# An attention and expert kernel whose 1,080 steps are issued in another written-down order

## The chip, the cores and the metric

The kernel runs on one core of one Trainium2 chip. The metric is device time in microseconds (us), the median of three runs.

## What is computed

Eight batches; in each, eight heads of 576 tokens with 64 channels go through two attentions, whose results are added, and the sum goes through a layer in which 128 chosen tokens pass an expert.

```python
def _attn_ref(q, k, v):
    # q_d, k_d, v_d: means over groups of 4 tokens (144 left)
    out_up = np.repeat(softmax(scale * q_d @ k_d.T) @ v_d, 4, axis=2)
    # every token attends to the tokens less than 4 places away
    scores = np.where(abs(pos[:, None] - pos[None, :]) < 4, scale * q @ k.T, -1e9)
    return out_up + softmax(scores) @ v

def _moe_ref(x, w_gate, w1, w2, capacity):     # x: 8 x 576 x 512
    scores = x @ w_gate
    for b in range(8):
        top = the 128 tokens of b with the highest scores
        out[b, top] = x[b, top] + sigmoid(scores[b, top]) * (relu(x[b, top] @ w1) @ w2)
```

## The kernel before

The work is cut into 1,080 steps. A step belongs to one engine (PE, DVE, ACT, POOL, or SP for loads and stores) and emits a few instructions. `Plan.add` collects them batch by batch, `Plan.given` (L216) reads the table `ORDER` (L40), and `Plan.emit` emits the steps in that order. Every engine takes its instructions strictly in the order in which they were emitted, and so does each queue of transfers. So the table decides, engine by engine, what stands behind what. The entry `54+4` is step 54 with four idle matmuls ahead of it (`idle`, L269): products of an identity matrix into the step's own bank, which no result uses. Since the table is there, the planner in `Plan.order` does not run, and the numbers that the steps carry (times in ns, `key`, `size`) have no effect.

One batch b goes through these parts:

- **Loads.** `load_qk` loads q and k (`T`, two transfers of 1152 KB, two buffers in turn) and DVE sums groups of four (`dT`). `load_vw` loads the windows of v (`vw`), `pool_v` loads v once more (`vraw`) and POOL sums it.
- **Coarse attention** (`coarse`, L513). PE makes scores (`sd`), ACT the exponentials (`ed`, `er`), PE turns them (`pspd`, `pspr`) and multiplies (`od`, step `products`), DVE scales (`ods`), SP writes that to memory (`up_d`) and reads it back spread fourfold into `up`, one transfer step for each of five tiles j.
- **Local attention** (`local`, L676), in three pieces k of two, two and one tiles. PE makes scores (`sl`), DVE the maxima (`mx`, `mb`), PE subtracts them (`sl` out of `minus`), ACT the exponentials (`ex`), PE turns them (`pspl`), ACT copies (`pt`), PE multiplies (`ol`), DVE divides (`t`), POOL adds `up` (`t` out of `t,up`), DVE takes the gate's sum (`jk`), SP stores the tokens (`out_dram` out of `t`).
- **Route** (`route`, L859). With all five sums there (`scp`), PE spreads them (`sb`), DVE compares (`beat`) and PE counts (`cb`), DVE writes the choice (`oh`), PE picks the indices (`pi`), DVE makes them whole numbers (`idx`). Then POOL issues a gather of the 128 chosen rows from memory (`xe` out of `out_dram,idx`, L933); it needs `idx` and the landed stores of that batch. PE turns the rows (`px`), ACT and DVE split them into two halves (`xeh`, `xel`).
- **Experts** (`experts`, L965). PE multiplies by w1 (`ph`, 96 matmuls in eight steps), ACT and DVE cut and split (`hh`, `hl`), PE multiplies by w2 (`py`, 24 matmuls in eight steps), DVE adds (`xe` out of `py`), POOL scatters the rows back.

The weights come once: eight loads into `stg` (two buffers in turn, shared with `w_gate`), each split by ACT (`w1h`, `w2h`) and DVE (`w1l`, `w2l`); a load waits until DVE has done with the buffer's load before. All instructions of steps stand under line L89, since the wrapper there records them; so they are told apart by their tiles.

```python
for st in self.given() if ORDER else self.order():
    for b in st.makes:
        b.tile = b.make()
    for _ in range(st.fills):
        self.idle(st.fill)
    st.emit()
```

Of the kernel before, what the change touches and what calls it, by code (L numbers as in the profile page):

```python
# [21 lines left out]
P = 128  # L22
# [15 lines left out]
ACCUM, OT = True, False  # L38
BIASED = (2,)
ORDER = """  # L40
# [38 lines left out]
"""  # L79


# [41 lines left out]
class Plan:  # L123
# [11 lines left out]
    def add(self, engine, ns, key, emit, r=(), w=(), uses=(), claims=(), after=(), size=0, lock=False, fill=None, soft=()):  # L135
        step = Step(engine, ns, key, emit, r, w, uses, claims, after, size, lock, fill, soft)
        self.steps.append(step)
        return step
# [94 lines left out]
def tile_multires_attention_moe(ctx: ExitStack, tc: tile.TileContext, qk, vw, vp, cs, w_gate, w1, w2, outs):  # L233
# [8 lines left out]
    DM = H * D  # L242
# [34 lines left out]
    add = plan.add  # L277
# [4 lines left out]
    def small(tag, shape, dtype=F32):  # L282
        return Buf(tag, 3, lambda: sm.tile(list(shape), dtype, tag=tag, name=tag))

    def two_banks(name):
        return Buf("psA", 2, lambda: psA.tile([P, 2, 512], F32, tag="A", name=name))
# [5 lines left out]
    def fixed(t):  # L292
        b = Buf(None, 1, None)
        b.tile = t
        return b
# [33 lines left out]
    out_d = [fixed(None) for b in range(B)]  # L329
# [346 lines left out]
    def local(b, k, key):  # L676
        tiles = TU[k]
        T, vl, sc = Ts[b], vws[b][k], scs[b]
        ns = len(tiles)
        ng = ns * HP  # L680
        s = two_banks("sl")
# [43 lines left out]
        mx = small("mx", [P, 2, UL * HP])  # L725
        mb = None if biased else small("mb", [P, 2, UL * HP], BF16)
        given = biased and ACCUM
        dn = small("dn", [P, 2, UL * HP]) if given else None
        ex = sbuf("ex", [P, UL * HP, 2 * KW], 2)
# [31 lines left out]
        def row_exps(i):  # L761
            for g in range(HP * i, HP * (i + 1)):
                for a in range(2):
                    act.activation(
                        ex[:, g, KW * a : KW * (a + 1)], s[:, a, KW * g : KW * (g + 1)], AF.Exp,
                        bias=mx[:, a, g : g + 1], scale=scale, **({"accum_out": dn[:, a, g : g + 1]} if given else {}),
                    )
            if given and i == ns - 1:
                act.activation(dn[:, :, :ng], dn[:, :, :ng], AF.Copy, bias=EPS)
# [5 lines left out]
        if biased:  # L775
            add("ACT", 200, key, negative, r=[mx], w=[mx])
            for i in range(ns):
                add("ACT", (2325 + 190 * (i == ns - 1)) if given else 1592, key + 0.004 * i, lambda i=i: row_exps(i), r=[s, mx], w=[ex, dn] if given else [ex])
            row = ex.writers[:]
            if given:  # L780
                add("DVE", 165, key + 0.01, inverse, r=[dn], w=[dn])
        else:
            add("DVE", 95, key, low, r=[mx], w=[mb], lock=True)
            add("PE", 20 + 425 * ns, key, shift, r=[mx, mb, minus], w=[s])
            add("ACT", 60 + 440 * ns, key, exps, r=[s], w=[ex])
            row = ex.writers * ns
# [72 lines left out]
    def route(b, key):  # L859
# [59 lines left out]
        pi = bank("T" if b == B - 1 else "F", "pi")  # L919

        def pick():
            for j in range(NT):
# [7 lines left out]
        idx, gs = small("idx", [P, 1], I32), small("gs", [P, 1])  # L930
        add("DVE", 70, key + 0.02, lambda: vec.tensor_copy(idx.tile, pi[:, 0:1]), r=[pi], w=[idx])
        xe = sbuf("xe", [P, DM], 3)
# [1 line left out]
            "POOL", 1050, key + 0.02,  # L934
            lambda: pool.indirect_dma_start(
                out=xe.tile, out_offset=None, in_=x_d[b], in_offset=bass.IndirectOffsetOnAxis(ap=idx.tile, axis=0),
            ), r=[idx, out_d[b]], w=[xe], size=P * DM * 4,
        )
        def gates():
            act.activation(gs.tile, pi[:, 1:2], AF.Exp, scale=-1.0)  # L940
            act.activation(gs.tile, gs.tile, AF.Copy, bias=XS * WS * WS, scale=XS * WS * WS)

        add("ACT", 240, key + 0.03, gates, r=[pi], w=[gs])
        add("DVE", 165, key + 0.04, lambda: vec.reciprocal(gs.tile, gs.tile), r=[gs], w=[gs])
        px = bank("T", "px")

# [157 lines left out]
```

## Time and profile before

| | |
|---|---|
| median of three runs | 295.74 us (294.67 to 295.88) |
| the profiled execution | 297.18 us |
| its span, first to last instruction | 295.40 us |
| PE busy | 252.6 us, 86% |
| DVE busy | 218.1 us, 74% |
| ACT, POOL busy | 134.8 us, 126.7 us |
| moved by DMA | 70.4 MB, 238 GB/s over the span |
| mean granted TensorE clock | 0.975 |

The profile shows one execution, instruction by instruction. The windows view gives each engine's busy time in a stretch, the granted TensorE clock (1.00 is 2.4 GHz, 0.50 is 1.2 GHz) and the busy share of the 16 DMA engines. A timeline gives one engine's instructions with the idle time ahead of them and what ended it. The chain of waits is the work that ended last, followed back from the end. The profiled execution is 1.44 us above the median, 0.5%.

### The profile page before, as it was taken

The numbers are of one execution on the slowest core, as the hardware profiler recorded it, in microseconds if no ns is written. First come the engines' busy times: TensorE is split into PE (matmuls) and PEld (weight loads), VectorE is DVE, ScalarE is ACT, GpSimd is POOL, SyncE is SP. The second block draws the span as 40 slices with busy tenths as digits, with TensorE's granted clock in tenths as the row PEclk, the third lists the DMA queues.
The fourth block names the chain that finished last, engine by engine and source line by source line (L and its number), as shares of the span: only waits on it lengthen the run. The fifth ranks groups of instructions, "written<-read, shape, count | busy, mean of one in ns | idle before, by whom it ended". The sixth has DMA issues, their size and how long they took to land.

```text
span 295.4 us, 11752 instructions
## 1 busy us (share of the span) xinstructions
PE 252.6 (86%) x5000; PEld 184.0 (62%) x5000; DVE 218.1 (74%) x466; ACT 134.8 (46%) x474; POOL 126.7 (43%) x160
## 2 busy tenths in 40 slices
PE   3887896686499797999989759999999999997892
PEld 0654564464287467867775548867865787693571
DVE  2888798778489888988888888689895885387211
ACT  0388665364355544286415633645347453620110
POOL 6055838474212668255572731157414521082201
PEclk9999999759889999999999999999999999999999
DMA  7999986787959989987984897857837462645200
GB/s 229 387 416 359 350 307 194 251 285 243 345 185 314 273 305 358 306 311 224 329 291 157 249 366 246 299 167 187 285 121 224 136 170 73 198 117 165 71 2 36
DMA packets 27195, 70.40 MB, mean 238 GB/s; under 512 B 5864, under 2 KB 8040, under 8 KB 24328
## 3 DMA queue, kind: packets, MB, share of 16 engines
q1 hardware_dynamic: 25864, 65.47, 66.3%
q0 software_dynamic: 1280, 4.20, 4.1%
q8 instruction: 39, 0.64, 0.9%
q14 instruction: 12, 0.10, 0.1%
HBM read 55.76 MB, written 13.89 MB: 236 GB/s over the span
## 4 chain that ended last, share of the span: by engine, by line
PE 39%; DMA 16%; issue 8%; DVE 6%; SPq 4%; ACT 3%; POOL 2%; POOLq 0%; DVEq 0%; ACTq 0%
PE ph L89 8%; PE py L89 7%; DMA up<-up_d 7%; PE sl L89 6%; DMA xe<-out_dram,idx 5%; SPq L89 4%; PE ol L89 4%; PE od L89 4%; PE pspl L89 3%; POOL t L89 2%; ACT ex L89 2%; PE sd L89 2%; PE pspd L89 2%; DMA vw<-in_vw_dram 2%; PE sb L89 2%
## 5 line engine op out<-in xcount | busy, mean ns | idle before, releaser
L89 POOL TENSOR_TENSOR t<-t,up 128x512 f32<-128x512 f32 x40 | 50.2, 1272 | 56.6 <-DMA up<-up_d 35.9
L89 PE MATMUL ph<-xel,w1h 128*128 128x128 f16 x256 | 44.2, 219 | 0.5 <-DVE xel L89 0.5
L89 PE MATMUL ph<-xeh,w1h 128*128 128x128 f16 x256 | 44.3, 219 | 0.0
L89 PE MATMUL ph<-xeh,w1l 128*128 128x128 f16 x256 | 44.2, 219 | 0.0
L89 DVE TENSOR_REDUCE dT<-T 128x288 f32<-128x1152 f32 (+3 forms) x31 | 42.0, 1379 | 2.7 <-DMA T<-in_qk_dram 2.7
L89 PEld LDWEIGHTS <-w1h 128*128 128x128 f16 x512 | 39.2, 98 | 1.6 <-issue 0.3
L89 ACT COPY pt<-pspl 128x512 f32<-128x512 f32 x40 | 22.9, 585 | 31.1 <-PE pspl L89 30.9
L89 PE MATMUL ol<-vw,pt 64*64 64x65 f32 x1280 | 27.8, 227 | 8.8 <-DMA vw<-in_vw_dram 4.3
L89 PEld LDWEIGHTS ol<-vw,pt 64*64 64x64 f32 x1280 | 22.9, 137 | 16.9 <-ACT pt L89 3.8
L89 DVE SCALAR_TENSOR_TENSOR jk<-t,wgp 128x512 bf16<-128x512 f32 x40 | 27.3, 682 | 4.8 <-POOL t L89 3.9
L89 POOL DMA_INDIRECT xe<-out_dram,idx x8 | 9.1, 1136 | 47.8 <-DVE idx L89 15.4
L89 DVE TENSOR_REDUCE mx<-sl 128x16 f32<-128x1024 f32 (+1 forms) x24 | 25.0, 1042 | 4.5 <-PE sl L89 4.1
L89 PE MATMUL pspl<-cst,ex 128*128 128x128 f32 x160 | 25.3, 284 | 2.3 <-ACT ex L89 1.8
L89 PEld LDWEIGHTS sl<-T 64*58 64x58 f32 (+1 forms) x1280 | 23.5, 136 | 3.5 <-DMA T<-in_qk_dram 1.9
L89 DVE SCALAR_TENSOR_TENSOR beat<-sb,scp,first 128x640 bf16<-128x640 f32 (+4 forms) x40 | 22.9, 610 | 3.8 <-PE sb L89 2.1
L89 PEld LDWEIGHTS <-w1l 128*128 128x128 f16 x256 | 25.0, 98 | 0.6 <-issue 0.6
L89 PE MATMUL sl<-T 64*58 64x64 f32 (+1 forms) x1280 | 24.3, 225 | 1.2 <-DMA T<-in_qk_dram 0.8
L89 PE MATMUL py<-w2h,hh 128*128 128x512 f16 x64 | 24.4, 381 | 0.0
L89 PE MATMUL py<-w2l,hh 128*128 128x512 f16 x64 | 24.3, 379 | 0.0
L89 PE MATMUL py<-w2h,hl 128*128 128x512 f16 x64 | 24.3, 379 | 0.0
L89 ACT ACTIVATE ed<-sd,mxd 128x144 f32<-128x144 f32 x64 | 23.5, 379 | 0.8
L89 DVE TENSOR_TENSOR t<-ol,den 128x512 f32<-128x512 f32 x32 | 22.1, 691 | 1.1
(111 smaller groups left out, 516.3 us busy)
## 6 DMA issues: line engine op xcount, KB each, us to landing
T<-in_qk_dram SPq DMA_DIRECT2D x14, 1152.0 KB
vraw<-in_vp_dram SPq DMA_DIRECT2D x8, 1152.0 KB
up<-up_d SPq DMA_DIRECT2D x72, 120.0 KB
vw<-in_vw_dram SPq DMA_DIRECT2D x16, 520.0 KB
out_dram<-t SPq DMA_DIRECT2D x32, 192.0 KB
stg<-in_moe_w_dram SPq DMA_DIRECT2D x8, 512.0 KB
vw<-in_vw_dram SPq DMA_DIRECT2D x8, 260.0 KB
up_d<-ods SPq DMA_DIRECT2D x8, 256.0 KB
```

The source lines that it names most:

```text
L89: return lambda *a, **k: self.tc.keep_in_program_order(f(*a, **k))
```

## The change

The table `ORDER` is another one; it holds the same 1,080 steps. It has 55 idle matmuls where the old one has 40. Three numbers that only the planner reads are changed too. The table has one line fewer, so line numbers behind it are one lower.

```diff
 ORDER = """
-0 4 16 1 6 18 102 20 5 23 26 10 170 173 11 17 54+4 55 24 72 56 57 73 58 74 21 75 19 65 76 59 66 60 67+1 22 61 68 77 27
...
+0 1 5 16 18 11 9 2 20 6 23 26 7 10 24 170 173 54+6 55 56 17 25 57 72 58 65 73 59 60 74 19 75 66 67 76 68 83+1 61 21 27
...
-                add("ACT", (2325 + 190 * (i == ns - 1)) if given else 1592, key + 0.004 * i, lambda i=i: row_exps(i), r=[s, mx], w=[ex, dn] if given else [ex])
+                add("ACT", (2325 + 290 * (i == ns - 1)) if given else 1592, key + 0.004 * i, lambda i=i: row_exps(i), r=[s, mx], w=[ex, dn] if given else [ex])
...
-            ), r=[idx, out_d[b]], w=[xe], size=P * DM * 4,
+            ), r=[idx, out_d[b]], w=[xe], size=P * DM * 12,
...
-        add("ACT", 240, key + 0.03, gates, r=[pi], w=[gs])
+        add("ACT", 300, key + 0.03, gates, r=[pi], w=[gs])
```

**First place: PE around the turn of batch 0's gathered rows (`px`).** Before:

```order
L89 MATMUL sl<-mb,minus 128x512
L89 MATMUL pspl<-cst,ex 128x128 x4
L89 LDWEIGHTS identb
L89 MATMUL px<-identb 128x512
L89 MATMUL px<-cst,xe 128x128 x4
L89 MATMUL od<-vd,ptd 64x64 x16
L89 MATMUL od<-vr,ptr 128x256 x2
L89 MATMUL od<-vd,pz_88 32x64 x8
L89 MATMUL od<-vd,ptr 128x64
L89 MATMUL sb<-cst,scp 128x128 x5
L89 MATMUL pspl<-cst,ex 128x128 x4
```

Now:

```order
L88 MATMUL sl<-mb,minus 128x512
L88 MATMUL pspl<-cst,ex 128x128 x4
L88 MATMUL od<-vd,ptd 64x64 x16
L88 MATMUL od<-vr,ptr 128x256 x2
L88 MATMUL od<-vd,pz_88 32x64 x8
L88 MATMUL od<-vd,ptr 128x64
L88 MATMUL pspl<-cst,ex 128x128 x4
L88 MATMUL px<-cst,xe 128x128 x4
L88 MATMUL ol<-vw_963,pt 64x65 x16
L88 MATMUL sb<-cst,scp 128x128 x5
```

The coarse product `od` of batch 2 and one turn `pspl` stood behind `px` and now stand ahead of it; the idle matmul ahead of `px` is gone. A little further up, a block of local scores (`sl` out of `T`) has moved from ahead of batch 0's `pi` to behind it, and `pspr` and one `pspd` the other way.

**Second place: PE around the turn of batch 3's gathered rows.** Before:

```order
L89 MATMUL cb<-ones,beat 128x1
L89 MATMUL px<-cst,xe 128x128 x4
L89 LDWEIGHTS beat
L89 MATMUL cb<-ones,beat 128x1
L89 LDWEIGHTS beat
L89 MATMUL cb<-ones,beat 128x1
L89 LDWEIGHTS identb
L89 MATMUL sl<-mask,identb 64x512
```

Now:

```order
L88 MATMUL cb<-ones,beat 128x1
L88 MATMUL pspl<-cst,ex 128x128 x8
L88 LDWEIGHTS minus
L88 MATMUL sl<-mx,minus 128x512
L88 LDWEIGHTS minus
L88 MATMUL sl<-mb,minus 128x512
L88 LDWEIGHTS minus
L88 MATMUL sl<-mx,minus 128x512
L88 LDWEIGHTS minus
L88 MATMUL sl<-mb,minus 128x512
L88 MATMUL px<-cst,xe 128x128 x4
L88 LDWEIGHTS oh
```

A block of local scores of batch 5, two turns `pspl` and one subtraction now stand ahead of `px`, which comes just before the next batch's pick. Above that, `pspr` and `pspd` of batch 5 have moved from behind batch 4's `sb` to ahead of it.

**Third place: SP's queue between the last loads of weights and batch 2's read-back (`up` out of `up_d_96`).** `t_853` is batch 1's last piece, `t_666` its middle piece; the `T` here is batch 3's. Before:

```order
L89 DMA out_dram<-t_853 6x512
L89 DMA T<-in_qk_dram 128x2304
L89 DMA up_d_96<-ods 128x512
L89 DMA stg<-in_moe_w_dram 128x2x512
L89 DMA out_dram<-t_666 48x2x512
L89 DMA out_dram<-t_666 10x2x512
L89 DMA out_dram<-t_666 48x2x512
L89 DMA out_dram<-t_666 10x2x512
L89 DMA vw_1489<-in_vw_dram 128x1040
L89 DMA up_81<-up_d_96 60x1x512 x2
L89 DMA T<-in_qk_dram 128x2304
```

Now:

```order
L88 DMA up_d_96<-ods 128x512
L88 DMA up_d_96<-ods 8x16x64
L88 DMA stg<-in_moe_w_dram 128x2x512
L88 DMA T<-in_qk_dram 128x2304
L88 DMA out_dram<-t_853 48x512
L88 DMA out_dram<-t_853 10x512
L88 DMA out_dram<-t_853 48x512
L88 DMA out_dram<-t_853 6x512
L88 DMA T<-in_qk_dram 128x2304
L88 DMA up_81<-up_d_96 60x1x512 x4
```

The first `T` of batch 3 and batch 1's last stores stood ahead of the write of `ods` and of the last `stg` load; now they stand behind both.

On POOL, batch 0's gather stood behind the four additions of batch 1 that come first; now three of these four stand behind the gather. On SP, the last store of batch 0 stood behind four read-back steps of batch 1 and one `vraw` load; now it stands behind two of them and no `vraw` load. On PE, batch 6's expert steps and batch 7's route end the table in nearly the old order; ahead of the last `px` there are ten idle matmuls instead of four, and one `py` step fewer stands between the last pick and that `px`.

## Rows read from the trace of the kernel before

**Rows 1.** The page's first part: busy us, share, instructions.

```profile
PE 252.6 (86%) x5000; PEld 184.0 (62%) x5000; DVE 218.1 (74%) x466; ACT 134.8 (46%) x474; POOL 126.7 (43%) x160
```

**Rows 2.** Windows: stretch, length, PE, PEld, DVE, ACT, POOL, clock, DMA, GB/s.

```profile
75.00:80.00 5.00, 0.78 (x3) 0.41 (x3) 2.53 (x5) 1.27 (x3) 1.26 (x1) 0.93 0.97 331
80.00:83.00 3.00, 3.00 (x40) 2.46 (x38) 1.46 (x4) 2.25 (x3) 0.07 (x1) 0.55 1.04 395
90.00:130.00 40.00, 36.25 (x765) 26.74 (x763) 36.38 (x74) 20.70 (x82) 20.98 (x23) 1.00 0.92 313
170.00:178.00 8.00, 5.02 (x138) 4.17 (x134) 5.94 (x20) 3.28 (x8) 2.69 (x7) 1.00 0.98 362
178.00:262.00 84.00, 82.11 (x1721) 63.17 (x1711) 63.37 (x145) 40.10 (x145) 30.46 (x36) 1.00 0.60 187
```

**Rows 3.** The chain of waits: start us, us, what.

```profile
72.24 7.31 DMA xe<-out_dram,idx
...
96.14 6.88 DMA up<-up_d
...
167.79 8.75 DMA xe<-out_dram,idx
...
183.09 2.44 PE od L89 x54
```

**Rows 4.** PE's timeline, 66 to 86 us: start, us, what, [idle <-its end].

```profile
75.83 0.38 PE L89 MATMUL px<-identb 128*128 128x512 bf16 x1 [1.02 <-ACT pt L89]
79.59 1.12 PE L89 MATMUL px<-cst,xe 128*128 128x128 f32 x4 [3.39 <-DMA xe<-out_dram,idx]
...
84.43 0.60 PE L89 MATMUL pspl<-cst,ex 128*128 128x128 f32 x4
```

**Rows 5.** DVE's timeline, 64 to 100 us.

```profile
69.48 0.14 DVE L89 CAST idx<-pi 128x1 int32<-128x1 f32 x1
...
81.38 0.69 DVE L89 SCALAR_TENSOR_TENSOR xel<-px,xeh 128x512 f16<-128x512 f32 x1 [3.48 <-ACT xeh L89]
...
84.08 0.76 DVE L89 TENSOR_TENSOR ods<-od,dend 128x576 f32<-128x576 f32 x1 [1.21 <-PE od L89]
...
87.36 0.61 DVE L89 SCALAR_TENSOR_TENSOR beat<-sb,scp,first 128x384 bf16<-128x384 f32 x1
```

**Rows 6.** POOL's timeline, 44 to 80 us.

```profile
72.24 1.96 POOL L89 DMA_INDIRECT xe<-out_dram,idx  x1 [2.72 <-DMA out_dram<-t]
```

**Rows 7.** SP's timeline, 56 to 108 us (the issues, not the transfers).

```profile
78.81 0.37 SPq L89 DMA_DIRECT2D T<-in_qk_dram  x1
84.87 0.35 SPq L89 DMA_DIRECT2D up_d<-ods  x1
87.47 0.38 SPq L89 DMA_DIRECT2D stg<-in_moe_w_dram  x1
87.95 1.66 SPq L89 DMA_DIRECT2D out_dram<-t  x4
...
90.17 2.15 SPq L89 DMA_DIRECT2D up<-up_d  x2
```

**Rows 8.** PE's timeline, 164 to 182 us.

```profile
172.40 0.73 PE L89 MATMUL sb<-cst,scp 128*128 128x128 f32 x5 [1.39 <-DVE scp L89]
...
176.68 0.63 PE L89 MATMUL px<-cst,xe 128*128 128x128 f32 x4 [1.32 <-DMA xe<-out_dram,idx]
...
177.50 1.07 PE L89 MATMUL sl<-T 64*58 64x64 f32 x64
```

**Rows 9.** PE's timeline, 264 to 279 us.

```profile
265.06 0.81 PE L89 MATMUL py<-identb 128*128 128x512 bf16 x3
265.71 0.38 PE L89 MATMUL py<-w2h,hh 128*128 128x512 f16 x1
...
272.27 0.53 PE L89 MATMUL pi<-vals,oh 128*128 128x2 bf16 x15 [0.34 <-DVE oh L89]
...
276.76 0.66 PE L89 MATMUL px<-cst,xe 128*128 128x128 f32 x4 [0.49 <-DMA xe<-out_dram,idx]
```

73 rows, old and new, of the table ORDER are left out of this document.

## Prediction

> **What bounds the kernel now.** I read the page's busy shares first: PE is busy 86% of the span, DVE 74%, nothing else above half [rows 1]. So PE is the first suspect, and the question is where it stands still. The windows answer it: from 178 to 262 us PE is busy 82.11 of 84 us [rows 2]; there nothing but less work on PE would help, and any time that PE gains earlier comes through to the end unless what feeds it falls behind. Before that there are holes. In 75 to 80 us PE works 0.78 of 5 us, in 170 to 178 us 5.02 of 8 [rows 2]. The chain of waits names what ends them: the gather of batch 0's chosen rows, 7.31 us from 72.24, and that of batch 3, 8.75 us from 167.79 [rows 3]. PE's timeline shows who is held: `px`, the turn of the gathered rows, stands in PE's queue ahead of work that needs no gather, and all of it waits [rows 4, 8]. Between the two holes, in 90 to 130 us, PE (36.25 of 40) and DVE (36.38) are nearly full together while the DMA engines are at 0.92 [rows 2], so in that stretch three things bind almost equally.
>
> **The change part by part.** The steps are the same, so busy time stays, save for 15 more idle matmuls. What changes is which work lies beside which wait.
>
> *Batch 0's gather.* Before `px` PE waits 1.02 us, then, after one idle matmul, 3.39 us [rows 4]: 4.41 us. Now `od` of batch 2 and a `pspl` stand ahead of `px`. An `od` step takes 2.44 us at full clock [rows 3], and 3.4 here (from the end of `px` at 80.71 [rows 4] until `ods` could start at 84.08 [rows 5]); `pspl` takes 0.60 [rows 4]. A block `sl` (1.07 for its products [rows 8]) has come between `pi` and `px`, a `pspd`, four matmuls like that `pspl`, 0.60, has left. That is 2.44 + 0.60 + 1.07 - 0.60 = 3.5 us more cover, 4.5 us with the slow `od`. The gather may also start sooner. Its indices were made at 69.62 us (69.48 plus 0.14 [rows 5]), but it went out at 72.24, released by the landing of batch 0's last stores [rows 6]. Those stores now stand behind less on SP: up to 2.6 us more. Cover and start together exceed 4.41, so I take the whole wait: **-4.4**, bounds -4.4 and 0 (0 if the gather slips by what the cover gains).
>
> Can DVE follow? In the same place it idles 3.48 us ahead of `xel` and 1.21 ahead of `ods` [rows 5], 4.69 us, both behind the held `px`. So it can follow a gain of 4.4, not much more.
>
> *The clock.* In 80 to 83 us the granted clock is 0.55, that is 1.2 GHz for nearly all of it, and it fell after the 0.78 busy us of the stretch before [rows 2]. At that clock `od` took 3.4 instead of 2.44, and `px` 1.12 instead of 0.63 to 0.66 [rows 4, 8, 9]: about 1.4 us. If the hole closes, this may go too. I take half, **-0.7**, bounds -1.4 and 0.
>
> *Batch 3's gather and batch 4's route.* PE waits 1.32 us for the gather and 1.39 for `scp` ahead of batch 4's `sb` [rows 8]. Now a block `sl` (1.07 at least [rows 8]) and two turns stand ahead of that `px`, more than 1.32, and `pspr` with a `pspd` (0.60, as above) ahead of `sb`. **-1.3 - 0.6 = -1.9**, bounds -2.7 and 0.
>
> *Moved transfers.* The last `stg` load, batch 3's `T`, batch 1's last stores and the five read-back steps of batch 2 now form one row on SP. What it waits for is `ods` of batch 2, and that came at 84.84 us only because its `od` was held behind `px`: SP stood from 79.18 to 84.87 [rows 7]. This wait shortens with the first term. But what is asked for 4 to 5 us earlier must also arrive earlier, and the engines are at 0.92 already [rows 2]; a read-back here took 6.88 us [rows 3]. I let a part of the gain be given back to transfers: **+1.0**, bounds 0 and +2.2 (half of the first term).
>
> *Idle matmuls.* Three take 0.65 us (265.06 to 265.71 [rows 9]), 0.22 each. Most of the new ones stand in the first 75 us, where PE waits anyway; three more ahead of batch 0's first `py` and three ahead of a `pspr` of batch 5 may cost, 0.65 for the first. Ahead of the last `px` there are now ten: after the last `pi`, which ends at 272.80 [rows 9], three `py` steps of 0.65 (eight rows of three matmuls 0.22 apart as in [rows 9]) and ten times 0.22 make 4.1 us, while the gather lets `px` start 3.96 us after `pi` [rows 9]. So 0.1 there. **+0.8**, bounds 0 and +1.5. All other moves lie beside work on a fuller engine, and I cost them at nothing: the additions of batch 1 that now stand behind the gather on POOL wait longer, but batch 1's route starts only when PE and DVE have passed `px` and `xel`.
>
> The sum is -4.4 - 0.7 - 1.9 + 1.0 + 0.8 = **-5.2 us**. From the profiled execution's 297.18 that gives 292.0. That execution is 1.44 above the median; so for the median I say 295.74 - 5.2 = **290.5 us**. All bounds on the good side give -8.5, 287.2; a shorter wait of SP and of the reads behind it, which I did not price, could add 2, 285.2. All on the bad side give +3.7, 299.4.
>
> **A rule against it.** The trace shows the two gathers at 7.31 and 8.75 us with the DMA engines at 0.97 and 0.98 [rows 2, 3], and at the quiet end `px` starts 3.96 us after `pi` [rows 9]; how long a gather takes hangs on what else is being moved. The Trainium skill, "DMA: Bandwidth & Descriptors", section "Anatomy of one DMA — SWDGE (gpsimd) path", fits a transfer from GpSimd as about 2.0 us plus its bytes over 436 GB/s, by which a gather of 256 KB would take an estimated 2.6 us, more cover would be worth nothing, and the first and third terms would go: +1.1, 296.8. The trace contradicts that fit under load, so it gets no chance of its own.
>
> **The rivals.**
>
> *Transfers bind.* Asked for earlier, the loads do not come earlier; PE and DVE run into `up`, `T` or `vw` instead of `px`. For it: 0.92, 0.97 and 0.98 of the DMA engines before 178 us. Against it: 313 GB/s in 90 to 130, while 395 were moved in 80 to 83 [rows 2]. Most of the first term is given back, 1.4 of it stays, and the third term halves: -1.4 - 1.0 + 0.2 = -2.2, 293.5 us.
>
> *Nothing changes.* The holes close at `px` and open at the next thing in line (`scp`, `pt`, `vw`), as 1.39 us for `scp` already stand beside the gather's 1.32 [rows 8]; the idle matmuls take what is left. Within 1 us of 295.7. Against it: at 75 to 80 us PE, DVE and POOL were all idle at once [rows 2], and all for one gather.
>
> *SP's row turns against it: slower.* The last `stg` load waits for DVE to have done with an earlier load; in DVE's new order that comes after `xel` of batch 0 and three compares instead of two, 0.61 us more [rows 5]. Before, that load went out at 87.47; batch 3's `T` went out at 78.81, ahead of it [rows 7]. If batch 0's gather is no earlier than it was, the load goes at 88.1, `T` 9.7 us later than now, then batch 1's stores, and the read-back, which went at 90.17 [rows 7] and lies on the chain [rows 3], 3.0 us later (0.61, then the issue of `T` 0.37, of four stores 1.66 and of the second `T` 0.37 [rows 7]). With +0.8 for the idle matmuls and -1.3 left of the third term: +2.5, 298.2 us. It decides at 87.5 us: each us by which that load is earlier takes one off, and I expect it about 4 us earlier. A gather that POOL holds longer, with batch 1's additions behind it, would start the same chain.
>
> That the change does not do what it says cannot be: the order shown is the one that is issued.
>
> **How the numbers follow.** A change of 0.5% (1.5 us) is about what a measurement here can tell from none. Forecast 0.52, transfers 0.20, nothing 0.12, slower 0.16. Faster is forecast and transfers, 0.72; same 0.12; slower 0.16. The range 285.5 to 297.5 takes in the good side's end, transfers and nothing; it leaves out most of the slower case and a little beyond the good end. Given faster, I expect 286 to 294.
>
> **What would show it.** Right: `px` of batch 0 waits under 1 us and starts by 77; the clock is not at 0.5 just behind it; SP writes batch 2's `ods` by 80; batch 4's `sb` starts by 168; PE stays full up to the last product, and the stretch from the last `pi` to the end keeps its length. Wrong: PE full and no earlier by 178 us, new waits on `up`, `vw` or `T` of more than 3 us, the last `stg` load after 87.5, or new holes behind a gather that POOL holds.

## The result, and the profile after

The changed order takes 299.46 us (median; 296.59 to 300.39) against 295.22 us (294.67 to 295.88) of the old one: ratio 1.0116, interval 1.0068 to 1.0164, so 2.0 to 4.8 us slower. The forecast was 290.5 us, faster. The profiled execution of the new order took 299.85 us, its span is 297.7. Ratios compare fast executions alone (those within 1.5% of their kernel's fastest), and six of the later profiles (few_idle, vw_early, early_old, early_old_sp, late_new, t_late_again) are of slow ones and are used for no comparison of stretches.

The page's first part, as [rows 1]:

```profile
PE 255.4 (86%) x5015; PEld 183.5 (62%) x5015; DVE 218.2 (73%) x466; ACT 135.5 (46%) x474; POOL 124.9 (42%) x160
```

PE has the 15 more idle matmuls, the rest is the same. The windows, in the columns of [rows 2], two stretches added (130 to 150 and 135 to 140):

```profile
75.00:80.00 5.00, 3.83 (x90) 2.83 (x84) 2.37 (x6) 2.45 (x6) 3.73 (x3) 1.00 0.71 194
80.00:83.00 3.00, 2.04 (x32) 1.94 (x33) 2.65 (x9) 0.87 (x1) 2.15 (x5) 1.00 0.92 247
90.00:130.00 40.00, 37.99 (x712) 26.03 (x714) 35.19 (x71) 22.43 (x90) 22.07 (x23) 1.00 0.90 310
130.00:150.00 20.00, 15.72 (x360) 12.53 (x352) 14.58 (x30) 7.98 (x23) 8.76 (x12) 0.94 0.87 274
135.00:140.00 5.00, 2.64 (x144) 2.28 (x139) 2.68 (x6) 0.37 (x3) 4.04 (x5) 1.00 0.91 295
170.00:178.00 8.00, 5.42 (x98) 3.53 (x95) 6.49 (x17) 2.21 (x5) 3.88 (x9) 1.00 0.99 359
178.00:262.00 84.00, 80.37 (x1671) 61.70 (x1672) 60.91 (x143) 40.99 (x146) 28.93 (x35) 1.00 0.63 199
```

The hole that the forecast aimed at is closed (3.83 of 5 us instead of 0.78), and PE is fuller in 90 to 130 us. Then a new hole stands at 135 us, and in the stretch that was full before, 178 to 262, PE does 1.7 us less. PE's timeline at the places that matter (as [rows 4, 8, 9]):

```profile
78.17 0.63 PE L88 MATMUL px<-cst,xe 128*128 128x128 f32 x4 [0.60 <-DMA xe<-out_dram,idx]
...
80.64 0.73 PE L88 MATMUL sb<-cst,scp 128*128 128x128 f32 x5 [1.21 <-DVE scp L88]
...
138.90 0.39 PE L88 MATMUL sl<-T 64*58 64x64 f32 x11 [2.21 <-issue]
...
147.01 0.56 PE L88 MATMUL od<-vd,ptd 128*64 128x64 f32 x10 [1.92 <-issue]
...
172.95 0.69 PE L88 MATMUL pspr<-cst,erx 128*128 128x128 f32 x2 [1.59 <-POOL erx L88]
173.65 0.76 PE L88 MATMUL sb<-cst,scp 128*128 128x128 f32 x5
...
180.27 0.60 PE L88 MATMUL px<-cst,xe 128*128 128x128 f32 x4
...
214.75 0.70 PE L88 MATMUL ol<-vw,pt 64*64 64x65 f32 x32 [1.23 <-DMA vw<-in_vw_dram]
...
274.63 0.53 PE L88 MATMUL pi<-vals,oh 128*128 128x2 bf16 x15 [0.34 <-DVE oh L88]
...
279.12 0.60 PE L88 MATMUL px<-cst,xe 128*128 128x128 f32 x4
```

Batch 0's `px` waits 0.60 us, batch 3's `px` and batch 4's `sb` nothing. New are two waits with no named releaser ("issue") inside batch 4's local scores and its `od`, one for POOL's `erx` ahead of batch 5's `pspr`, and one for batch 6's `vw`. The last `px` stands 4.49 us behind the last `pi`, exactly as before [rows 9], in spite of ten idle matmuls. POOL's timeline at batch 0's gather, and the addition of batch 1 behind it:

```profile
69.53 1.97 POOL L88 DMA_INDIRECT xe<-out_dram,idx  x1 [3.69 <-DMA stg<-in_moe_w_dram]
71.54 1.27 POOL L88 TENSOR_TENSOR t<-t,up 128x512 f32<-128x512 f32 x1
```

SP's timeline, at the row of [rows 7] and later:

```profile
82.10 1.45 SPq L88 DMA_DIRECT2D up_d<-ods  x2
84.68 0.41 SPq L88 DMA_DIRECT2D stg<-in_moe_w_dram  x1
...
88.87 1.73 SPq L88 DMA_DIRECT2D up<-up_d  x2
...
199.48 1.55 SPq L88 DMA_DIRECT2D out_dram<-t  x4
201.60 0.37 SPq L88 DMA_DIRECT2D vw<-in_vw_dram  x1
202.06 1.52 SPq L88 DMA_DIRECT2D out_dram<-t  x4
203.62 0.36 SPq L88 DMA_DIRECT2D T<-in_qk_dram  x1
205.35 2.73 SPq L88 DMA_DIRECT2D out_dram<-t  x4
208.12 1.35 SPq L88 DMA_DIRECT2D vw<-in_vw_dram  x2
```

The last `stg` load goes out at 84.68, so the slower rival's condition (after 87.5) did not come about. But batch 6's first `vw`, the first of the two in the last row shown, goes out at 208.12, behind two stores (202.06 and 205.35) that wait for POOL's additions and a `T`. In the old order it went at 202.40, right behind the store that stands at 199.48 here and ahead of those two:

```profile
200.76 1.55 SPq L89 DMA_DIRECT2D out_dram<-t  x4
202.40 0.92 SPq L89 DMA_DIRECT2D vw<-in_vw_dram  x1
```

### The profile page after: what moved, and what is told of

It is laid out like the page before. It is cut to its first block, busy times and chain, and to the rows that moved or that the text cites. A ratio compares the mean times of both kernels' runs of the same rounds, so it can differ in the third digit from the quotient of the medians.

```text
span 297.7 us, 11776 instructions
## 1 busy us (share of the span) xinstructions
PE 255.4 (86%) x5015; PEld 183.5 (62%) x5015; DVE 218.2 (73%) x466; ACT 135.5 (46%) x474; POOL 124.9 (42%) x160
## 4 chain that ended last, share of the span: by engine, by line
PE 40%; DVE 19%; issue 13%; DMA 11%; SPq 7%; POOL 5%; ACT 4%; POOLq 0%; DVEq 0%
PE sl L88 9%; SPq L88 7%; PE py L88 6%; PE od L88 5%; PE ph L88 5%; PE ol L88 4%; PE pspl L88 4%; POOL t L88 4%; DVE dT L88 3%; DMA up<-up_d 3%; DVE t L88 3%; DVE mx L88 3%; DMA T<-in_qk_dram 3%; DVE beat L88 3%; DVE jk L88 2%
## 5 line engine op out<-in xcount | busy, mean ns | idle before, releaser
L88 PE MATMUL ol<-vw,pt 64*64 64x65 f32 x1280 | 27.1, 223 | 5.9 <-ACT ex L88 2.3
L88 PEld LDWEIGHTS ol<-vw,pt 64*64 64x64 f32 x1280 | 22.2, 134 | 13.9 <-ACT pt L88 4.1
L88 PE MATMUL sl<-T 64*58 64x64 f32 (+1 forms) x1280 | 22.4, 215 | 2.2 <-issue 2.2
L88 PEld LDWEIGHTS sl<-T 64*58 64x58 f32 (+1 forms) x1280 | 22.0, 127 | 3.5 <-issue 2.5
L88 PEld LDWEIGHTS pspl<-cst,ex 128*128 128x128 f32 x160 | 18.1, 144 | 8.3 <-ACT ex L88 5.0
```

The costliest lines, as they stand in the source:

```text
L88: return lambda *a, **k: self.tc.keep_in_program_order(f(*a, **k))
```

## The experiments

Each kernel is another `ORDER`. "First 470 new" means the first 470 entries of the new table, then all steps that are left, in the sequence of the old one. Ratios are to the old order run beside the kernel; the old order itself ran from 292 to 302 us there. The medians are of all executions. By these the old order beside again has 297.83 us and beside new_again 297.01, so that the new order lies 0.8% and 0.7% above it: that it is slower is better known than by how much.

| kernel | ratio, interval | median of all, us |
|---|---|---|
| before_again (old) | 1.0002, 0.9958 to 1.0046 | 295.61 |
| again (new) | 1.0206, 1.0123 to 1.0288 | 300.06 |
| new_again (new) | 1.0124, 0.9982 to 1.0265 | 299.16 |
| new_then_old | 1.0041, 0.9969 to 1.0113 | 297.60 |
| old_then_new | 1.0224, 1.0143 to 1.0304 | 301.42 |
| mid_new | 1.0154, 1.0078 to 1.0230 | 301.24 |
| px_only | 1.0226, 1.0160 to 1.0292 | 300.49 |
| early_old | 1.0158, 1.0082 to 1.0234 | 302.67 |
| early_new | 0.9963, 0.9915 to 1.0011 | 296.56 |
| od_first | 0.9957, 0.9899 to 1.0015 | 296.61 |
| vw_early | 1.0087, 1.0034 to 1.0140 | 298.28 |
| vw_store_early | 1.0066, 1.0020 to 1.0113 | 298.56 |
| early_old_sp | 1.0106, 1.0056 to 1.0156 | 299.69 |
| few_idle | 1.0106, 1.0040 to 1.0172 | 300.18 |
| t_late | 1.0126, 1.0032 to 1.0221 | 297.89 |
| t_late_again | 1.0038, 0.9994 to 1.0081 | 297.44 |
| t_early | 1.0243, 1.0132 to 1.0354 | 302.78 |
| late_new | none (295.26 to 303.55) | 301.30 |

To see where time goes, I measured each of the other profiles against its own work. PE's products without idle matmuls, at full clock, are cut at the amounts of work that the first old profile had done by 125, 145, 168, 190 and 225 us. What a kernel needs from cut to cut, less that work, is what it lost there to waits, idle matmuls and the lower clock (us; o or n says whose order stands in a stretch, none where it is mixed):

```
                 to 125   125-145  145-168  168-190  190-225  225-end
first old         38.6 o    0.0 o    2.1 o    4.1 o    0.7 o   12.5 o
before_again      36.4 o    0.4 o    1.4 o    4.0 o    0.6 o   12.7 o
mid_new           35.8 o    1.9 n    1.2 n    5.4 o    0.6 o   13.3 o
new_then_old      34.6 n    1.7 o    1.3 o    5.7 o    0.5 o   11.8 o
px_only           37.1      0.1 o    1.6 o    3.7 o    1.6 o   12.4 o
early_new         37.7      0.0 o    1.8 o    3.1 o    0.6 o   13.0 o
od_first          36.2      1.4 o    0.1 o    4.5 o    0.8 o   13.2 o
t_early           37.5 o    0.0 o    7.6      5.0 o    0.6 o   12.9 o
old_then_new      38.6 o    1.9 n    2.0 n    3.1 n    3.7 n   12.8 n
first new         35.2 n    2.4 n    4.6 n    3.5 n    2.8 n   11.7 n
again             39.4 n    2.5 n    1.0 n    2.7 n    2.9 n   12.4 n
new_again         37.0 n    2.7 n    1.3 n    2.3 n    2.4 n   12.1 n
vw_store_early    38.2 n    1.8 n    1.6 n    3.2 n    0.9     12.6 n
t_late            36.6 n    4.0      1.8 n    2.3 n    1.0     12.1 n
```

**The two orders again.**

> The old order, word for word. All theories: the time of the kernel before, 293 to 299 us. It gives a second profile of the old order: how much of PE's waits (the 3.39 us for the gather of batch 0, 1.32 and 1.39 us at batch 3's px and batch 4's sb) and of the stretches at half the granted clock (13.6 us of them in the first profile) belong to the order. If they do, they are there again within 1 us each; if they are an accident of one execution, they are not, and terms of the prediction that were read from them were read from an accident.

> The changed order, word for word, once more. Theory A (the gain at batch 0's gather is real and is lost later): the median stays between 296.5 and 300; PE has done some 5 us more work than the old order by 120 us of the profile and has lost it by 150. Theory A1, a part of A: in the first profile PE stood 2.21 us in the middle of batch 4's local scores at 136.7 us and 1.92 us in the middle of batch 4's coarse product at 145.1 us, with nothing named that it waited for; an instruction load of 16 KB had just begun at both places. If that belongs to this order, the new profile shows idle time without a named releaser of 1.5 us or more between 130 and 150 us again. If it is an accident of one execution, the new profile has none there and a span under 295 us. Theory B (transfers give back every gain): the same time, but no such idle time; PE's waits between 120 and 150 us are for up, T or vw.

> The changed order, word for word, a third time, for the same chip and the same runs of the old order. All theories: 1 to 2 per cent over the old order. Theory K: a wait without a named releaser of 1 us or more in batch 4's local scores or coarse product; batch 6's first ol waits 1.2 to 2.4 us for vw.

The second old profile has a shorter hole ahead of batch 0's `px`, without the 1.02 us for `pt`:

```profile
75.98 0.66 PE L89 MATMUL px<-cst,xe 128*128 128x128 f32 x4 [1.59 <-DMA xe<-out_dram,idx]
```

Five old profiles of the place show 1.3 to 3.4 us for the gather there: 3.39 was the largest. With the wait for `pt` the first has 4.41 us, the other four 1.6 to 3.7. In new_again the hole without a releaser is there (2.3 us in batch 4's local scores), and `ol` waits 1.03 us for `vw`; in again `ol` waits 1.83, and in place of the first hole PE waits 0.77 and 0.95 for DVE's `mx` and `mb`. The lead of some 1 us that again had over the first old profile by 90 us was gone by 110. The wait for `vw` belongs to the order; the hole at 135 us came in two of three.

**Heads and tails.**

```diff
-first 1080 of one table
+new_then_old: first 470 new, the rest old
+old_then_new: first 470 old, the rest new
+mid_new: 470 old, to 620 new, the rest old
+late_new: first 620 old, the rest new, with the two SP steps of vw_store_early
```

> The first 470 steps in the new order (to about 124 us), all the others in the old order among themselves. Theory A (gain real, the new order after 124 us loses it): the lead of 4 to 6 us at 120 us stays, 290.0 to 292.0 us, 3 to 5 us under the old order. Theory B (transfers give it back, whatever order follows): 294.5 to 296.5 us, and by 150 us PE has no more work done than in the old order. Theory C (the ten more idle matmuls of this head cost what they last): 2 us above A's time, 292 to 294.

> The first 470 steps in the old order, all the others in the new order among themselves. Theory A: this tail has a cost of its own behind 150 us (batch 4's first store stands on SP behind the write of batch 5's ods, so batch 4's gather went out at 193.44 instead of 183.01 us): 297 to 299.5 us, 2 to 4 us over the old order, the loss between 170 and 220 us; whether instruction loads come late between 125 and 150 us here is open, each such hole adds 2 us. Theory B: the order behind 124 us does not matter by itself, 294.5 to 296.5 us.

> The old order, but steps 470 to 620 of the list (about 125 to 168 us) in the new order. Theory D (the tail of the new order loses where batch 5's pspr with three idle matmuls stands ahead of batch 4's sb, and where instruction loads come late, 130 to 180 us): 1.5 to 3 us over the old order. Theory E (the tail loses behind 185 us, by loads and stores that were put later on SP): within 1 us of the old order.

> The old order to step 620 of the list (about 168 us), then the new order, with batch 6's first vw and batch 4's first store in their old places. If the third term of the forecast (batch 3's gather and batch 4's route, -1.9 us, bounds -2.7 and 0) is real and only the other places ate it: 1.0 to 2.0 us under the old order, the best of the kernels so far. If it is not: the old order's time within 0.7 us.

The new head brings nothing that the times can tell (1.0041), against theory A's 3 to 5 us; the new tail costs what the whole change costs (1.0224). mid_new shows part of it (theory D; 1.9 us in its second column, and 6.8 us at half clock behind a hole at 170). late_new has no ratio and settles nothing, so the third term has no run of its own.

**The first 80 us.**

```diff
-... 116 350 145+1 236 241 120 328 255 ...
+... 116 350 328 145 236 241 120 255 ...     (od_first: the old table with od, 328, ahead of px, 145)
+px_only: 210 old, to 280 new, the rest old
+early_old: first 200 old, the rest new
+early_new: first 200 new, the rest old
```

> The old order, but with the steps between about 60 and 80 us in the new order, so that batch 0's px stands behind batch 2's od and a pspl; SP's row of the last stg load, batch 3's T and batch 2's read-back stays as it was. Theory A: px waits under 1 us and PE is 3 to 4.5 us ahead of the old order at 90 us; with SP's row as it was a part is lost until 130 us: 291.0 to 293.5 us. Theory B: PE is ahead at 90 us and not at 130 us, 294.5 to 296.0 us. The rival that was forecast as slower (SP's row): no effect here, since that row is the old one.

> The first 200 steps (to about 58 us) in the old order, all the others in the new order among themselves. Theory F (the new order loses in its first 60 us, which were costed at nothing: PE's time without useful work by 60 us was 18.2 to 21.1 us in five profiles that begin in the old order and 22.9 to 23.7 in five that begin in the new one): 2.5 to 4.5 us under the new order, 295 to 297 us here. Theory G (a late start is taken up by the wait for batch 0's gather, which is there either way): within 1 us of the new order.

> The first 200 steps in the new order, all the others in the old order among themselves: the mirror image. Theory F: 2 to 4 us over the old order. Theory G: within 1 us of the old order, with the wait at batch 0's px shorter by what was lost before.

> The old order with one PE step moved: batch 2's coarse product od (2.44 us at full clock) stands ahead of batch 0's px instead of behind it, and the idle matmul ahead of px is gone. Nothing else moves on any engine or queue. This is the forecast's first term alone. If that term is worth what it was given (-4.4 us, of which od covers 2.44): px waits 0.3 to 1.3 us less cover left, 2.0 to 2.5 us under the old order. Theory G (the wait at px is slack that the rest of the kernel takes up: transfers and DVE set the pace until 125 us): the wait at px is shorter by 2 us or more and the time is that of the old order within 0.7 us.

px_only, early_old and early_old_sp do not test what they were made for. In the new order ACT has the splits of two weight loads ahead of an `ex`; with the old start these loads come later, ACT stands, and PE waits 3.5 to 6.5 us for `ex`. px_only's ACT timeline:

```profile
73.08 1.06 ACT L88 ACTIVATE w2h<-stg 128x1024 f16<-128x1024 f32 x1 [9.32 <-DMA stg<-in_moe_w_dram]
```

early_new is even with the old order or a little under it: theory G, not F. od_first is the forecast's first term alone, one step moved. Its PE and DVE timelines:

```profile
79.20 0.63 PE L88 MATMUL px<-cst,xe 128*128 128x128 f32 x4 [0.66 <-DMA xe<-out_dram,idx]
82.13 1.02 PE L88 MATMUL sb<-cst,scp 128*128 128x128 f32 x5 [2.31 <-DVE scp L88]
```

```profile
80.49 0.69 DVE L88 SCALAR_TENSOR_TENSOR xel<-px,xeh 128x512 f16<-128x512 f32 x1 [2.03 <-ACT xeh L88]
81.10 0.68 DVE L88 SCALAR_TENSOR_TENSOR jk<-t,wgp 128x512 bf16<-128x512 f32 x1
81.70 0.08 DVE L88 DVE_READ_ACCUMULATOR jk<-t,wgp 128x1 f32 x1
81.82 0.17 DVE L88 TENSOR_TENSOR scp<-sc,cst 128x5 f32<-128x5 f32 x1
```

`od` hides its part of the gather, `px` waits 0.66 us, and 2.31 us come back at once at batch 1's `sb`: on DVE batch 1's last `jk` stands behind `xel`, which needs the gathered rows too. The five old profiles show no wait at that `sb`. The hole has moved one step. The time (0.9957) agrees with a gain of 0 to 3 us, so theory G and a part of the term are both left open.

**SP's moved steps, and idle matmuls.**

```diff
-... 745 554 773 ... 860 756 827 672 ...
+... 745 827 554 773 ... 860 756 672 ...     (vw_early; 827 loads batch 6's first vw)
-... 641 823 626 ... 735 615 766 ...
+... 641 615 823 626 ... 735 766 ...         (vw_store_early has both; 615 stores batch 4's first tokens)
-54+6 233+7 128+3 343+3 160+4 716+3 1055+10
+54+4 233+3 128 343+1 160+1 716 1055+4       (few_idle)
+early_old_sp: early_old with both SP steps moved
```

> The new order with one SP step moved: the load of batch 6's first vw window stands right behind the store of batch 5's k0i1j1 again, as in the old order, ahead of two stores that wait for POOL's additions and of batch 7's T. Theory E: batch 6's first ol, which waited 1.23, 1.83 and 2.43 us for vw in three profiles of the new tail and not at all in the old one, waits under 0.3 us; 1.0 to 2.5 us under the new order. Theory D: the wait is filled by the next thing in line, same time within 0.7 us.

> As vw_early, and batch 4's first store (k0i1j1) stands ahead of batch 6's second T load on SP, as in the old order, instead of behind the write of batch 5's ods. Theory E: batch 4's gather goes out by 184 us instead of 193.4, its px by 191 instead of 199; 2 to 4 us under the new order, near the old order's time. Theory D: the gather is earlier and the time is that of the new order within 0.7 us.

> The first 200 steps in the old order, the others in the new one, and the two SP steps of batch 6's vw and batch 4's first store in their old places. Theories E and F together: the two costs add, so 3.5 to 6.5 us under the new order, 293 to 295.5 us here, 1 to 3 under the old order, since only the gain at batch 0's gather is left. If both costs are real but the gain is not, the time of the old order within 1 us.

> The new order with 32 idle matmuls instead of 55 (7 to 3 ahead of batch 1's first ol that waits, 6 to 4 at the start, 10 to 4 ahead of the last px, none ahead of batch 0's sb and batch 5's pspr, 1 each ahead of batch 2's first pspl and batch 0's first py). Theory C (they cost what the forecast said, 0.8 us, or up to 1.5): 0.8 to 1.5 us under the new order. Theory H (they stand in waits and cost nothing): within 0.5 us of it. If they hold the clock up: a lower granted clock before 80 us and a longer time.

vw_store_early's PE timeline has no wait ahead of that `ol`, and its POOL timeline the gather ten us earlier than 193.44:

```profile
211.32 0.70 PE L88 MATMUL ol<-vw,pt 64*64 64x65 f32 x32
```

```profile
182.96 1.04 POOL L88 DMA_INDIRECT xe<-out_dram,idx  x1 [9.51 <-DVE dT L88]
```

From 190 to 225 us it loses 0.9 us instead of 2.4 to 3.7: theory E. The ratios fall with it, though their intervals overlap those of the new order; batch 4's store adds nothing that can be told. few_idle lies within the spread of the new order: what the 23 idle matmuls cost does not show. Theory C's 0.8 to 1.5 us would be 0.3 to 0.5%, less than its interval can tell, so C and H are not decided.

**The hole at 135 us.** The transfers' view has a queue q8 of instruction loads of 16 KB; there are 39 (0.64 MB). They follow PE's 5,015 matmuls and as many weight loads, one for each 256 of them in all 20 profiles, so I take them for PE's. In the new order's first profile none begins between 126.5 and 136.2 us, where one queue alone moved anything:

```profile
q1 hardware_dynamic: 848, 3.35, 101.3%
```

The next one begins at 136.33; PE stops at 136.69, the load has landed at 137.38, and PE goes on at 138.90; the view of 136.2 to 138:

```profile
DMA packets 245, 0.49 MB, mean 271 GB/s; under 512 B 52, under 2 KB 52, under 8 KB 233
...
q8 instruction: 1, 0.02, 3.7%
```

The traces settle that PE waits for this load. In the 20 profiles, 20 waits of PE without a releaser last over 0.5 us. 18 of them stand at places of PE's sequence that lie whole multiples of 256 matmuls and weight loads apart, give or take one, and PE goes on 1.2 to 1.7 us after the last such load has landed. The loads begin late when the DMA engines are full: from the place in PE's sequence where the earliest of them begin it takes an estimated 0.7 us (median) with the engines under 0.3 busy in the next 3 us, and 3.4 above 0.95.

Five of the six compared profiles with the new order there show 1.4 to 2.3 us of it, seven with the old order at most 0.4. The old order has a lull of the DMA engines in the same place:

```profile
135.00:140.00 5.00, 5.00 (x118) 4.21 (x115) 4.72 (x9) 2.91 (x12) 2.75 (x4) 1.00 0.64 172
```

```diff
-... 411 691 409 693 492 692 ... 502 503 516 695 517 ... 425 694 623 ...
+... 411 691 409 492 692 ... 502 503 693 516 517 ... 425 694 695 623 ...   (t_late, on vw_store_early; 693 loads T)
-... 409 465 410 ... 599 297 693 600 ...
+... 409 465 693 410 ... 599 297 600 ...                                   (t_early, on the old table)
```

> The kernel vw_store_early (the new order with batch 6's first vw and batch 4's first store in their old places) with one more edit: batch 5's second T load stands on SP behind batch 3's k1i1j3 store, about 12 us later, as it did in the old order, and DVE's sum that reads it stands next to its partner. Theory K (in 125 to 147 us the new order leaves the DMA engines no lull, so PE's instruction loads of 16 KB come 6 to 8 us late, and PE stands 1.1 to 2.2 us in batch 4's local scores): the wait without a named releaser in that step falls under 0.6 us, 1 to 2 us under vw_store_early. Theory L (PE's instruction loads are late there for another reason, such as more instructions per us): the wait of 1.1 to 2.2 us is there again, same time as vw_store_early within 0.7 us.

> The old order with one SP step moved: batch 5's second T load goes out behind the third read-back step of batch 3, about 5 us earlier, into the lull of the DMA engines between 135 and 140 us (172 GB/s there in the old order against 295 to 342 in the new). Theory K: in batch 4's local scores or coarse product PE now stands 0.7 to 2 us with no named releaser, as in the new order, where four profiles of this place in the old order show at most 0.4 us; 0.5 to 2 us over the old order. Theory L: no such wait, the time of the old order within 0.7 us.

> t_late, word for word, once more. In its first profile PE's wait without a named releaser in batch 4's local scores was gone, but DVE took 2.58 us over one small mb (0.17 us elsewhere) while POOL ran two additions, and PE waited 2.16 us for that. Theory K (the late instruction loads cost what they last): no such wait without a releaser again; without DVE's long mb 0.5 to 1.0 per cent over the old order. Theory M (another wait always takes the place): PE loses 1.5 us or more between 130 and 150 us again, under whatever name.

In t_late the lull is back and the hole without a releaser is gone, and PE loses as much in the next step; its windows, PE, DVE and POOL:

```profile
135.00:140.00 5.00, 4.85 (x199) 4.22 (x200) 4.50 (x10) 2.51 (x10) 4.42 (x6) 1.00 0.69 210
```

```profile
143.62 0.58 PE L88 MATMUL sl<-mb,minus 128*128 128x512 bf16 x1 [2.16 <-DVE mb L88]
```

```profile
140.99 2.58 DVE L88 TENSOR_TENSOR mb<-mx 128x16 bf16<-128x16 f32 x1
```

```profile
141.05 2.48 POOL L88 TENSOR_TENSOR t<-t,up 128x512 f32<-128x512 f32 x2
```

DVE's `mb` starts with POOL's two additions and ends with them. The second profile of the kernel has the same 2.58 us; in again, which has no hole without a releaser, an `mb` of 1.29 us beside two additions stands in this place. t_early brought no hole of this kind, but it hardly tests theory K: its `T` went out only at 138.11 us, behind the row of read-backs, and the lull was there still (0.72). Batch 3's last read-back came late instead:

```profile
152.58 1.30 PE L89 MATMUL sb<-cst,scp 128*128 128x128 f32 x5 [4.51 <-DVE scp L89]
```

Where the old profiles show at most 1.3 us, 4.51. So theory M holds for both moves: what is moved out of one wait's way lands in another's. Of theory K the wait for the load is shown, and the hole went with the transfer in both profiles; it was not made to come.

## Why the prediction was wrong

- **Batch 0's gather, -4.4: the step that failed.** The cover came, the gain did not. `px` now waits 0.4 to 1.2 us in five of six new profiles (not at all in the sixth), and PE does the work that I counted as cover. But `px` starts no earlier: 78.2 to 80.8 us in these six, 76.0 to 79.6 in five with the old order; the sign "by 77" failed. Up to 125 us the loss is 36.8 us on average with the new head (the six marked n above, 34.6 to 39.4) and 37.4 with the old (the five marked o, 35.8 to 38.6): 0.6 us of gain, uncertain by an estimated 1.8 from the spread of these eleven. Four things are wrong in the step.
  - "I take the whole wait" took one execution's 4.41 us, the largest of five, for the order's. And `pspr` (0.52 us) left the cover beside `pspd`, so that 3.5 us more cover should have been 3.0.
  - The gather does not land earlier. The wait for the stores is gone, as forecast: it goes out 0.3 us after `idx` in all six new profiles. But `idx` is made at 69.2 to 71.8 us instead of 66.6 to 69.6, so the gather goes out at 69.5 to 72.1, as before (70.5 to 72.2). And the term's bound of 0 came true: the gather slipped. Where `px` waits for it, `px` starts 7.9 to 8.7 us after the gather goes out, instead of 5.3 to 7.4; its first packets begin 4.2 to 5.6 us after that instead of 2.0 to 3.4, with the DMA engines at 0.95 to 1.03 in 72 to 76 us in both orders.
  - The new order arrives later, by moves that I "cost at nothing". PE's waits in the first 60 us add up to 12.9 us in the first old profile and 15.4 in the first new one. Without idle matmuls and at full clock PE has done 44.9 us of work by 70 us on average in the five old profiles and 40.4 in the six new ones; by 84 us, behind the gather, it is 51.8 and 51.2. So about 4 us are won at the hole, and they were lost ahead of it.
  - It asked what covers the gather on PE and not who else needs the rows; in od_first, where only `od` moves, DVE's `xel` and with it batch 1's route wait for them. In the new order `scp` stands ahead of `xel`, and batch 1's `sb` still waits 0.5 to 1.2 us for it.

  How much each of these takes is not separated: in the runs with the new cover and the old start (px_only, early_old, early_old_sp) ACT stands instead.
- **The clock, -0.7.** At 75 to 83 us it is 1.00, as hoped, but in the new profile 3.4 us at 1.2 GHz, from 147.5 us, follow the two holes instead (0.94 in 130 to 150).
- **Batch 3's gather and batch 4's route, -1.9: right by this count.** 168 to 190 us loses 2.85 us on average with the new order (2.3 to 3.5 in six profiles) and 4.44 with the old (3.1 to 5.7 in eight): -1.6. The wait at `px` is gone in all six, that at `sb` is at most 0.56; 1.59 and 0.94 for `erx` came for them in two profiles. The sign "`sb` by 168" failed (173.65 us in the first new profile): PE came there no earlier.
- **Moved transfers, +1.0.** SP's row ran 1.3 to 2.8 us earlier (`ods` at 82.10, not by 80), the rival's condition did not come. Its 3.0 us were also summed wrongly: four stores stood between that load and the read-back before as well, so their 1.66 us are no addition, and one `vw` left; about 1.0 us is right. The price was elsewhere, by places that I cost at nothing: +1.7 us on average in 125 to 145 (2.2 against 0.5) and +2.2 in 190 to 225 (3.0 against 0.8; a `vw` that I had not seen behind the stores).
- **Idle matmuls, +0.8:** few_idle cannot tell it from nothing. From the last `pi` to the last `px` it takes as long as before, as forecast.

With 145 to 168 (1.9 against 1.4 us, the 4.6 of one profile among them) and 225 to the end (12.3 against 12.7) the means add up to -0.6 + 1.7 + 0.5 - 1.6 + 2.2 - 0.4 = +1.8 us, just under the measured 2.0 to 4.8. So in this count the two places, 125 to 145 and 190 to 225, account for the sign; that what is left is chance is not shown. Of the two, vw_store_early undoes the second, and what t_late takes out of the first comes back beside it. The outcome was the slower rival's by sign, by another mechanism; "transfers bind" came nearest in kind: earlier work ran into late loads.

The rule of the Trainium skill, "DMA: Bandwidth & Descriptors", section "Anatomy of one DMA — SWDGE (gpsimd) path", by which I estimated 2.6 us for a gather, did not decide anything: batch 3's gather still took 8.38 us from issue to landing.

## What to carry to other kernels

A hole in the profile is worth what remains after the next consumer of the late thing has been looked for on every engine; move the one step alone before believing in its price. In a new written order cost every stretch, the start above all, and look on each queue for a load that now stands behind a store that waits. When one run differs from the next by 1%, read the wait in several profiles before pricing it.

## What was not expected of the hardware

PE can stand for 1.4 to 2.3 us with no releaser that the profile names, while the DMA engines are full and a load of its own instructions comes late. And a DVE operation of 0.17 us took 2.58 beside POOL's additions. The Trainium skill, "SBUF — State Buffer", section "SBUF: two separate sides", says that DVE and GpSimd share a port pair as an exclusive lock: a DVE operation with two SBUF inputs and a GpSimd operation that reads SBUF take it for the whole instruction, and the one that comes second is held. The traces agree. `mb`, whose two inputs lie in SBUF, took at most 0.18 us in all 239 executions (20 profiles) with no POOL operation beside it, and over 0.48 in 41 of the 81 with one. They show it held for several additions in a row: two in t_late, four in few_idle (4.21 us) and vw_early (4.84). Which came first in t_late is not shown, since `mb`'s record begins 0.06 us ahead of POOL's. An addition of batch 1 that the new order puts right behind batch 0's gather on POOL holds an `mb` for 1.1 to 1.3 us in all six new profiles and in none of the five old ones; what that costs was not measured.
